# Two attention heads' blocks in one decode step: one row of the last weight matrix loaded ahead of the others, in uneven transfers

## The chip, the core and the metric

The kernel runs on one core of a Trainium2 chip. The time is device microseconds (us) of one execution, as the median of several runs; lower is better. A core has TensorE (PE, matrix products), VectorE (DVE), ScalarE (ACT), GpSimd (POOL), SyncE (SP, which here only issues transfers) and sixteen DMA engines that carry all transfers from the large memory (HBM) into the on-chip memory of 128 partitions.

## What is computed

Two independent attention blocks, A and B, each for one new token. Both have 32 query heads, 16 heads of keys and values, 8192 cached positions of 128 numbers; A looks at the last 2048 positions only (W), B at all.

```
q = (x @ wq)                      # 576 -> 32 x 128
scores = q . k * 128**-0.5        # over W (A) or 8192 (B) cached positions
p = softmax(scores)
o = p . v                         # 32 x 128
out = o.reshape(4096) @ wo        # 4096 -> 576
return concat([out_A, out_B])     # 1152 numbers, bf16
```

The inputs are bf16. The cached keys and values of B are the bulk of the bytes: some 67 MB of the 102.76 MB that the kernel reads.

## The kernel before

The program is written as a list of operations for each engine, with named dependences; the class `Prog` turns these into semaphores. The order on each engine is the order in which the operations are put down.

**Loads.** All large loads are issued by SP, in one order, into one ring of 72 x 1024 bf16 per partition (`place`, L167 to L185). Each load has a semaphore of its own out of 24 (`s_ld`), and waits only until the piece of the ring that it overwrites has been used. A load of 128 partitions increments its semaphore sixteen times. The order is: wq of A and B (L189 to L194), keys and values of the eight units (four of A, four of B; L219 to L222), then wo of A and of B (L224 to L231). Apart from them, ACT loads the two vectors x (one row each, L253), and SP stores the two halves of the result (L523).

**Units.** A unit is four heads of keys and values. For each, DVE transposes keys in slabs (L350), PE multiplies them by the queries (L367), the maximum and the exponentials follow (L382 to L406), and PE multiplies the probabilities by the values (L431). The code of unit i puts the transposes and scores of unit i + 1 ahead of the products with the values of unit i.

**The end.** After the last unit the sums are folded and divided (L482 to L499); the result `oP` holds, for each block, 32 columns of 128 numbers. The last product, with wo, is at L502 to L524. wo has 4096 rows of 576 numbers; partition p holds rows 32p to 32p + 31, and these are called here row 0 to row 31 of wo (one row in each partition is 1152 bytes). For each row k there are two matmuls with a column of `oP` as weights: 320 columns of the result, and the other 256. They go to four separate bands of one PSUM bank (partitions 0 and 32 for A, 64 and 96 for B), and each band sums over its 32 rows. `NWO` (L34) says in what pieces wo is loaded and multiplied: A's in one of 32 rows, B's in pieces of 17, 8, 4, 2 and 1 rows. The pieces of B are called wo1.0 to wo1.4, and the multiplications F1.0 to F1.4; each F waits for its own piece. After the last row of a block ACT and DVE copy the two parts out of PSUM (L519, L521) and SP stores them.

Of the kernel before, what the change touches and what calls it, by code (L numbers as in the profile page):

```python
# [11 lines left out]
HQ = 32  # L12
G = 16
DH = 128
DM = 576
# [5 lines left out]
NQ = G // 4  # L21
# [9 lines left out]
RING = 72 * 1024  # L31
NSEM = 24
NKT = 3
NWO = [[32], [17, 8, 4, 2, 1]]  # L34


class Prog:
# [9 lines left out]
    def op(self, eng, fn, deps=(), name=None):  # L47
        self.ops[eng].append((fn, tuple(deps), name, None))
        if name is not None:
            assert name not in self.where, name  # L50
            self.where[name] = (eng, len(self.ops[eng]) - 1)

    def load(self, eng, fn, sem, value, deps=(), name=None, step=16):
        self.ops[eng].append((fn, tuple(deps), None, (sem, step)))
        if name is not None:
            assert name not in self.dma, name
            self.dma[name] = (sem, value)
# [40 lines left out]
def bass_concat_heads__sliding_block_cached__gqa_block_cached__decode_kernel(nc, A_x, A_k_cache, A_v_cache, A_wq, A_wo,  # L98
                         B_x, B_k_cache, B_v_cache, B_wq, B_wo, out):
    xs, ks, vs = [A_x, B_x], [A_k_cache, B_k_cache], [A_v_cache, B_v_cache]  # L100
    wqs, wos = [A_wq, B_wq], [A_wo, B_wo]
# [42 lines left out]
    oP = nc.alloc_sbuf_tensor("oP", [128, 2, HQ], BF16)  # L144
# [9 lines left out]
    def view(t, free, offset, dims, parts=128, p0=0):  # L154
        return bass.AP(tensor=t, offset=p0 * free + offset, ap=[[free, parts], *dims])

    pg = Prog(nc)
    op, load = pg.op, pg.load
    s_x = [nc.alloc_semaphore("s_x%d" % i) for i in range(2)]
    s_ld = [nc.alloc_semaphore("s_ld%d" % i) for i in range(NSEM)]  # L160
    s_out = nc.alloc_semaphore("s_out")
    s_row = [nc.alloc_semaphore("s_row%d" % i) for i in range(2)]

# [3 lines left out]
    def place(size, uses, issue, name):  # L167
        if at[0] + size > RING:
            at[0] = 0
        lo, hi = at[0], at[0] + size  # L170
        at[0] = hi
        deps = []
        for r in list(live):
            if r[0] < hi and lo < r[1]:
                deps += r[2]
                live.remove(r)
        n = nload[0]
        nload[0] += 1
        if n >= NSEM:
            deps += uses_of[n - NSEM]  # L180
        uses_of.append(list(uses))
        live.append((lo, hi, list(uses)))
        t = ring[:, lo:hi]
        load("sp", lambda e: issue(e, t), s_ld[n % NSEM], 16 * (n // NSEM + 1), deps=deps, name=name)
        return t  # L185
# [35 lines left out]
            if 0 <= n < NU:  # L221
                load_kv(kind, n)  # L222

    wo_at = {}  # L224
    for P in range(2):
        k0 = 0
        for c, kk in enumerate(NWO[P]):
            src = wos[P].rearrange("(p k) n -> p (k n)", k=HQ)[:, k0 * DM:(k0 + kk) * DM]
            wo_at[P, c] = place(kk * DM, ["F%d.%d" % (P, c)], lambda e, t, src=src: e.dma_start(t, src),
                                "wo%d.%d" % (P, c))  # L230
            k0 += kk  # L231

    def slab(kind, i, s):

# [9 lines left out]
       deps=["id0"], name="ident")  # L244
# [15 lines left out]
    for c in range(2):  # L260
        op("dve", lambda e, c=c: e.tensor_reduce(par[:, c:c + 1], view(identf, 128, c, [[2, 64]]), AX.X, ALU.add),
           deps=["identf"], name="par%d" % c)
# [3 lines left out]
    for P in range(2):  # L266
        op("dve", lambda e, P=P: e.tensor_copy(  # L267
            view(xdup, 256, 128 * P, [[2, 64], [1, 2]], parts=1),
            view(xrow, 2 * DM, P * DM + 512, [[1, 64], [0, 2]], parts=1)), deps=["x%d" % P], name="xd%d" % P)
        for k in range(5):  # L270
            def mm(e, P=P, k=k):
                if k < 4:
                    lhsT = view(xrow, 2 * DM, P * DM + k, [[4, 128]], parts=1)
                else:
                    lhsT = xdup[0:1, P, :]
                return e.matmul(banks[2 * P + k // 4][:, (k % 4) * 128:(k % 4 + 1) * 128], lhsT=lhsT,  # L276
                                rhs=onesb[0:1, :], start=True, stop=True)
            op("pe", mm, deps=["x%d" % P, "onesb", "xd%d" % P], name="xT%d.%d" % (P, k))
        op("dve", lambda e, P=P: e.tensor_copy(
            xrep[:, P, 0:4, :].rearrange("p k m -> p (k m)"), banks[2 * P][:, :]), deps=["xT%d.3" % P], name="xr%d.0" % P)  # L280
        for c in range(2):
            op("dve", lambda e, P=P, c=c: e.tensor_scalar(
                xrep[:, P, 4 + c, :], banks[2 * P + 1][:, 0:128], par[:, c:c + 1], None, ALU.mult),
                deps=["xT%d.4" % P, "par%d" % c], name="xr%d.%d" % (P, 1 + c))
# [3 lines left out]
       deps=["identf"], name="clsb")  # L288
    op("dve", lambda e: e.tensor_reduce(clsa[:], view(identf, 128, 0, [[1, 8], [8, 16]]), AX.X, ALU.add),
       deps=["identf"], name="clsa")  # L290
    op("dve", lambda e: e.tensor_reduce(sel[:], view(identf, 128, 0, [[1, 32], [32, 4]]), AX.X, ALU.add),
       deps=["identf"], name="sel")
# [6 lines left out]
    for P in range(2):  # L299
        for n in range(8):  # L300
            u = 8 * P + n
            bank = banks[u % 4]

            def mm(e, P=P, n=n, bank=bank):
                for k in range(5):
                    if k < 4:
                        lhsT, o = xrep[:, P, k, :], wq_at[P, 0][:, k * w + n * 512:k * w + (n + 1) * 512]
                    else:
                        lhsT, o = xrep[:, P, 4 + n // 4, :], wq_at[P, 1][:, (n % 4) * 512:(n % 4 + 1) * 512]
                    ins = e.matmul(bank[:, :], lhsT=lhsT, rhs=o, start=(k == 0), stop=(k == 4))  # L310
                return ins
            op("pe", mm, deps=["wq%d.0" % P, "wq%d.1" % P] + XR + (["qe%d" % (u - 4)] if u >= 4 else []),
               name="qmm%d.%d" % (P, n))
            op("act", lambda e, u=u, bank=bank: e.activation(qsb[:, u % 4, :], bank[:, :], ACT.Copy),  # L314
               deps=["qmm%d.%d" % (P, n)] + (["qT%d" % (u // 2 - 2)] if u >= 4 else []), name="qe%d" % u)
            if n % 2:
                op("dve", lambda e, u=u, n=n: e.transpose(  # L317
                    ktb[:, (n - 1) * 512:(n + 1) * 512].bitcast(I32),
                    qsb[:, u % 4 - 1:u % 4 + 1, :].rearrange("p a n -> p (a n)").bitcast(I32)),
                    deps=["qe%d" % (u - 1), "qe%d" % u] + (["z0.%d" % i for i in range(4)] if P else []),  # L320
                    name="qT%d" % (u // 2))
        for b in range(4):
            if P == 1:
# [3 lines left out]
                    deps=["qT%d" % u for u in range(4, 8)] + ["zb0"], name="z1.%d" % b)  # L327
            else:
# [3 lines left out]
                    deps=["qT%d" % u for u in range(4)] + ["za0"], name="z0.%d" % b)  # L332
# [4 lines left out]
    k0 = [sum(nslab[:i]) for i in range(NU)]  # L337
# [117 lines left out]
    for i in range(NU):  # L455
        n = nslab[i + 1] if i + 1 < NU else 0
# [18 lines left out]
        for s in range(nslab[i]):  # L475
# [13 lines left out]
                                start=True, stop=True),  # L489
       deps=["lsel", "lselA", "nb%d" % last, "mr%d" % last], name="L")  # L490
# [3 lines left out]
        deps=["rl", "O%d" % last], name="on")  # L494
    op("dve", lambda e: e.transpose(oq[:].rearrange("p c k -> p (c k)"), on[:].rearrange("p c k -> p (c k)")),
       deps=["on"], name="oq")
    op("pe", lambda e: e.matmul(mb[:, 64:128], lhsT=perm[:, :], rhs=oq[:].rearrange("p c k -> p (c k)"),
                                start=True, stop=True), deps=["oq", "rl", "perm"], name="pm")
# [2 lines left out]

    fb = qb[0]  # L502
    for P in range(2):
        k0 = 0
        for c, kk in enumerate(NWO[P]):
            def mm(e, P=P, c=c, k0=k0, kk=kk):
                for k in range(kk):
                    for n in range(2):
                        r, lo, hi = 32 * (2 * P + n), n * N0, N0 + n * (DM - N0)
                        ins = e.matmul(fb[r:r + 1, 0:hi - lo], lhsT=oP[:, P, k0 + k:k0 + k + 1],  # L510
                                       rhs=wo_at[P, c][:, k * DM + lo:k * DM + hi],
                                       start=(k0 + k == 0), stop=(k0 + k == HQ - 1))
                return ins
            op("pe", mm, deps=["wo%d.%d" % (P, c), "oP", "exp%d" % (NQ - 2)], name="F%d.%d" % (P, c))
            k0 += kk
        done = "F%d.%d" % (P, len(NWO[P]) - 1)
        r, lo = 64 * P, P * DM

        load("act", lambda e, r=r, lo=lo: e.activation(outsb[0:1, lo:lo + N0], fb[r:r + 1, 0:N0], ACT.Copy),  # L519
             s_row[P], 2, deps=[done], name="f%d" % P, step=1)  # L520
        load("dve", lambda e, r=r, lo=lo: e.tensor_copy(outsb[0:1, lo + N0:lo + DM], fb[r + 32:r + 33, 0:DM - N0]),  # L521
             s_row[P], 2, deps=[done], step=1)
        load("sp", lambda e, lo=lo: e.dma_start(out[0, 0:1, lo:lo + DM], outsb[0:1, lo:lo + DM]),  # L523
             s_out, 16 * (P + 1), deps=["f%d" % P], name="out%d" % P)  # L524
# [31 lines left out]
```

## Time and profile before

| | |
|---|---|
| median of 3 runs | 246.21 us (246.15 to 246.38) |
| span of the profiled execution, first to last instruction | 245.2 us |
| bytes read from HBM | 102.76 MB, 419 GB/s over the span |
| PE busy | 172.3 us, 70% of the span |
| DVE busy | 129.1 us, 53% |
| ACT busy | 24.3 us, 10% |
| SP's issue of wo of A | at 208.37 us |
| SP's issues of the five pieces of wo of B | from 208.74 us, 2.33 us in all |
| from issue to landing: wo of A, pieces of B | 23.9 us; 29.3, 31.6, 32.5, 32.8, 32.6 us |

The span is that of one execution taken with the hardware profiler; the median of the timed runs is 1.0 us longer, which is what lies around the first and the last instruction. Busy times are sums over the span; they say how much an engine did, not what the end waited for. A transfer's time from issue to landing includes its time in the queue behind the transfers ahead of it.

### The profile page before, as it was taken

To read this page: it belongs to the slowest core of one execution; us is meant where nothing else is said; L and a number is where in the kernel's file an instruction comes from. 1 tells how busy PE (TensorE), PEld (TensorE's weight loads), DVE (VectorE), ACT (ScalarE), POOL (GpSimd) and SP (SyncE) were. 2 spreads that over 40 slices of the span, in tenths; PEclk is the share of its full clock that TensorE was granted. 3 is DMA by queue.
4 is the path that set the end of the run, shared out by engine and by line. 5 is a ranking of instruction groups with operands and counts; after the bars stand their busy time and mean duration, and the time that the engine had idled before them with its cause. 6 is when DMAs were issued, how large, how long until landed. Compare 5 with 4: busy or idle time off the path is not lost.

```text
span 245.2 us, 2253 instructions
## 1 busy us (share of the span) xinstructions
PE 172.3 (70%) x960; PEld 71.8 (29%) x961; DVE 129.1 (53%) x162; ACT 24.3 (10%) x52; POOL 8.2 (3%) x15
## 2 busy tenths in 40 slices
PE   0269967787867994889582869945579939257197
PEld 0124422224433222432130523211423213213154
DVE  0422547667789986699501699810679920500201
ACT  2004540021201000100000100000010000200001
POOL 8400000000000000000000000000000000000000
PEclk9999995789999997569957578989657985677559
DMA  7999999999999999998999999999999999999994
GB/s 267 420 457 410 437 428 425 433 428 457 440 430 387 468 428 428 452 470 385 406 428 425 438 476 428 438 406 425 438 466 460 395 406 430 428 438 409 430 407 158
DMA packets 4481, 102.90 MB, mean 420 GB/s; under 512 B 500, under 2 KB 632, under 8 KB 1144
## 3 DMA queue, kind: packets, MB, share of 16 engines
q1 hardware_dynamic: 4468, 102.76, 97.9%
q8 instruction: 7, 0.11, 0.2%
q14 instruction: 2, 0.02, 0.0%
q10 hardware_dynamic: 4, 0.00, 0.0%
HBM read 102.76 MB, written 0.00 MB: 419 GB/s over the span
## 4 chain that ended last, share of the span: by engine, by line
DMA 55%; PE 29%; DVE 12%; ACT 2%; issue 2%; SPq 0%; DVEq 0%
DMA ring<-in_B_v_cache_dram 40%; DMA ring<-in_A_wo_dram 10%; DVE ktb L350 9%; PE vb L431 8%; DMA ring<-in_A_wq_dram 5%; PE qb L367 5%; PE qb L510 5%; PE sb L310 5%; PE qb L310 4%; ACT psb L406 1%; DVE pta L414 1%; PE ob L447 1%; PE sb L367 1%; PE qb L359 1%; PE mb L397 1%
## 5 line engine op out<-in xcount | busy, mean ns | idle before, releaser
L350 DVE STREAM_TRANSPOSE ktb<-ring 128x1024 int32<-128x1024 int32 x80 | 92.8, 1211 | 29.5 <-DMA ring<-in_B_k_cache_dram 28.3
L367 PE MATMUL sb<-ktb,zb 128*128 128x512 bf16 x256 | 76.0, 437 | 23.7 <-DVE ktb L350 21.1
L367 PEld LDWEIGHTS sb<-ktb,zb 128*128 128x128 bf16 x256 | 23.4, 106 | 72.4 <-DVE ktb L350 45.9
L431 PE MATMUL vb<-ring,pts 128*32 128x512 bf16 x256 | 24.7, 567 | 18.5 <-DMA ring<-in_B_v_cache_dram 14.4
L367 PE MATMUL qb<-ktb,za 128*128 128x512 bf16 x64 | 19.4, 449 | 2.8 <-DVE ktb L350 2.8
L431 PEld LDWEIGHTS vb<-ring,pts 128*32 128x32 bf16 x256 | 9.0, 134 | 33.6 <-DMA ring<-in_B_v_cache_dram 16.7
L438 ACT ACTIVATE xo<-vb 128x512 f32<-128x512 f32 x8 | 4.8, 597 | 129.4 <-PE vb L431 129.4
L418 DVE STREAM_TRANSPOSE pts<-psb 32x512 bf16<-32x512 bf16 x16 | 11.3, 703 | 9.5 <-ACT psb L406 9.3
L510 PE MATMUL qb<-ring,oP 128*1 128x256 bf16 (+1 forms) x128 | 11.3, 340 | 4.0 <-DMA ring<-in_A_wo_dram 4.0
L317 DVE STREAM_TRANSPOSE ktb<-qsb 128x512 int32<-128x512 int32 x8 | 5.7, 711 | 15.0 <-ACT qsb L314 15.0
L310 PE MATMUL sb<-ring,xrep 128*128 128x512 bf16 x40 | 11.4, 442 | 2.7 <-DMA ring<-in_A_wq_dram 2.7
L447 PEld LDWEIGHTS ob<-sel,xo 128*128 128x128 f32 x64 | 10.9, 244 | 3.8 <-ACT xo L438 2.2
L447 PE MATMUL ob<-sel,xo 128*128 128x8 f32 x64 | 10.1, 285 | 1.2 <-ACT xo L438 1.2
L367 PEld LDWEIGHTS qb<-ktb,za 128*128 128x128 bf16 x64 | 6.1, 109 | 13.4 <-issue 5.8
L310 PE MATMUL qb<-ring,xrep 128*128 128x512 bf16 x39 | 9.5, 393 | 0.0
L510 PEld LDWEIGHTS qb<-ring,oP 128*1 128x1 bf16 x128 | 7.0, 93 | 8.3 <-DMA ring<-in_A_wo_dram 4.1
L521 DVE CAST outsb<-qb 1x256 bf16<-1x256 f32 x2 | 0.8, 420 | 14.7 <-PE qb L510 14.7
L491 DVE RECIPROCAL rl<-mb 128x64 f32<-128x64 f32 x1 | 0.6, 558 | 12.3 <-PE mb L488 12.3
L276 PE MATMUL sb<-onesb,xrow 1*128 1x128 bf16 x4 | 0.6, 298 | 9.2 <-DVE xdup L267 9.2
L392 DVE TENSOR_REDUCE mr<-mb 1x8 f32<-1x128 f32 x8 | 1.9, 240 | 9.5 <-PE mb L384 9.5
L310 PEld LDWEIGHTS sb<-ring,xrep 128*128 128x128 bf16 x40 | 4.3, 109 | 8.6 <-issue 5.3
L314 ACT ACTIVATE qsb<-sb 128x512 bf16<-128x512 f32 x8 | 4.8, 597 | 19.1 <-PE sb L310 19.1
(65 smaller groups left out, 68.8 us busy)
## 6 DMA issues: line engine op xcount, KB each, us to landing
ring<-in_B_k_cache_dram SPq DMA_DIRECT2D x8, 4096.0 KB, 24.5
ring<-in_A_k_cache_dram SPq DMA_DIRECT2D x4, 2048.0 KB, 30.5
ring<-in_A_v_cache_dram SPq DMA_DIRECT2D x4, 2048.0 KB, 25.4
ring<-in_B_v_cache_dram SPq DMA_DIRECT2D x2, 4096.0 KB, 23.8
ring<-in_A_wo_dram SPq DMA_DIRECT2D x1, 4608.0 KB, 23.9
ring<-in_A_wq_dram SPq DMA_DIRECT2D x1, 4096.0 KB, 12.5
ring<-in_B_wq_dram SPq DMA_DIRECT2D x1, 4096.0 KB, 22.6
ring<-in_B_wo_dram SPq DMA_DIRECT2D x1, 2448.0 KB, 29.3
```

The lines of the kernel that those rows point to most:

```text
L310: ins = e.matmul(bank[:, :], lhsT=lhsT, rhs=o, start=(k == 0), stop=(k == 4))
L314: op("act", lambda e, u=u, bank=bank: e.activation(qsb[:, u % 4, :], bank[:, :], ACT.Copy), deps=["qmm%d.%d" % (P, n)] + (["qT%d" % (u // ...
L317: op("dve", lambda e, u=u, n=n: e.transpose(ktb[:, (n - 1) * 512:(n + 1) * 512].bitcast(I32), qsb[:, u % 4 - 1:u % 4 + 1, :].rearrange("p ...
L350: op("dve", lambda e: e.transpose(kt.bitcast(I32), src.bitcast(I32)), deps=[landed] + (["S%d" % (k - NKT)] if k >= NKT else Z), name="T%d. ...
L359: e.matmul(bank[:, :], lhsT=mkl[:].rearrange("p a h r -> p (a h r)"), rhs=mkr[:].rearrange("p q h -> p (q h)"), start=True, stop=False)
L367: ins = e.matmul(bank[:, :], lhsT=lhsT, rhs=view(ktb, KT, (k % NKT) * SLAB + 64 * c + v, [[128, 16], [2, 32]]), start=(side == "B" and s = ...
L397: op("pe", lambda e: e.matmul(mb[:, 128:129], lhsT=mexp[0:1, :], rhs=onesf[0:1, 0:1], start=True, stop=True), deps=["mx%d" % i, "ones"], n ...
L418: op("dve", lambda e, b=b: e.transpose(view(pts, NB * 128, 2 * b, [[8, 16], [128, NB], [1, 2]], 32, 32 * b), psb[32 * b:32 * b + 32, :]), ...
L431: ins = e.matmul(vbank[i][32 * j:32 * j + 32, :], lhsT=lhsT, rhs=src[:, 512 * j:512 * j + 512], start=(s == 0), stop=(s == nslab[i] - 1))
L438: op("act", lambda e: e.activation(xo[:, c, :], vbank[i][:, :], ACT.Copy), deps=["V%d.%d" % (i, nslab[i] - 1)] + (["O%d" % (i - 1)] if i e ...
L447: ins = e.matmul(ob[:, at:at + 8], lhsT=xo[:, c, 128 * t:128 * t + 128], rhs=sel[:, 8 * t:8 * t + 8], start=(t == 0), stop=(t == 3))
L510: ins = e.matmul(fb[r:r + 1, 0:hi - lo], lhsT=oP[:, P, k0 + k:k0 + k + 1], rhs=wo_at[P, c][:, k * DM + lo:k * DM + hi], start=(k0 + k == 0 ...
```

## The change

B's wo is cut into six pieces instead of five. The first is row 31 alone, and it is put ahead of the others in the queue; then rows 0 to 15, 16 to 23, 24 to 27, 28 and 29, and 30. The rows, the bytes and the matmuls are the same. Row 31 is loaded by three transfers, of the partitions 0 to 39, 40 to 124 and 125 to 127; the first has the semaphore that `place` gives, the other two have new ones (`s_wox`), and F1.0 waits for all three. The sum in each band now begins with row 31: `start` and `stop` go by a count of the rows done.

```diff
-NWO = [[32], [17, 8, 4, 2, 1]]
+NWO = [[32], [1, 16, 8, 4, 2, 1]]
+XWO = [(0, 40), (40, 125), (125, 128)]
...
+    s_wox = [nc.alloc_semaphore("s_wox%d" % i) for i in range(len(XWO) - 1)]
...
+        rows = wos[P].rearrange("(p k) n -> p (k n)", k=HQ)
         for c, kk in enumerate(NWO[P]):
-            src = wos[P].rearrange("(p k) n -> p (k n)", k=HQ)[:, k0 * DM:(k0 + kk) * DM]
-            wo_at[P, c] = place(kk * DM, ["F%d.%d" % (P, c)], lambda e, t, src=src: e.dma_start(t, src),
-                                "wo%d.%d" % (P, c))
-            k0 += kk
+            split = P == 1 and c == 0
+            wo_k[P, c] = HQ - 1 if split else k0
+            src = rows[:, wo_k[P, c] * DM:(wo_k[P, c] + kk) * DM]
+
+            def issue(e, t, src=src, part=XWO[0] if split else (0, 128)):
+                return e.dma_start(t[part[0]:part[1], :], src[part[0]:part[1], :])
+            t = wo_at[P, c] = place(kk * DM, ["F%d.%d" % (P, c)], issue, "wo%d.%d" % (P, c))
+            if split:
+                for i, part in enumerate(XWO[1:]):
+                    load("sp", lambda e, t=t, src=src, part=part: e.dma_start(
+                        t[part[0]:part[1], :], src[part[0]:part[1], :]), s_wox[i], 16, name="wox%d" % i)
+            else:
+                k0 += kk
...
-                                       start=(k0 + k == 0), stop=(k0 + k == HQ - 1))
+                                       start=(done + k == 0), stop=(done + k == HQ - 1))
...
+            op("pe", mm, deps=["wo%d.%d" % (P, c), "oP", "exp%d" % (NQ - 2)] +
+               ["wox%d" % i for i in range(len(XWO) - 1) if (P, c) == (1, 0)], name="F%d.%d" % (P, c))
```

More of the change, by code (lines that the diff above doesn't have):

```diff
@@ L222, in bass_concat_heads__sliding_block_cached__gqa_block_cached__decode_kernel @@
                 load_kv(kind, n)
-    wo_at = {}
+    wo_at, wo_k = {}, {}
     for P in range(2):
         k0 = 0
+        rows = wos[P].rearrange("(p k) n -> p (k n)", k=HQ)
         for c, kk in enumerate(NWO[P]):
-            src = wos[P].rearrange("(p k) n -> p (k n)", k=HQ)[:, k0 * DM:(k0 + kk) * DM]
-            wo_at[P, c] = place(kk * DM, ["F%d.%d" % (P, c)], lambda e, t, src=src: e.dma_start(t, src),
-                                "wo%d.%d" % (P, c))
-            k0 += kk
+            split = P == 1 and c == 0
[10 more added lines that the diff above has]
+                k0 += kk
     def slab(kind, i, s):
@@ L503, in bass_concat_heads__sliding_block_cached__gqa_block_cached__decode_kernel, with mm @@
     for P in range(2):
-        k0 = 0
+        done = 0
         for c, kk in enumerate(NWO[P]):
-            def mm(e, P=P, c=c, k0=k0, kk=kk):
+            def mm(e, P=P, c=c, k0=wo_k[P, c], kk=kk, done=done):
                 for k in range(kk):
@@ L511, in mm @@
                                        rhs=wo_at[P, c][:, k * DM + lo:k * DM + hi],
-                                       start=(k0 + k == 0), stop=(k0 + k == HQ - 1))
+                                       start=(done + k == 0), stop=(done + k == HQ - 1))
                 return ins
-            op("pe", mm, deps=["wo%d.%d" % (P, c), "oP", "exp%d" % (NQ - 2)], name="F%d.%d" % (P, c))
-            k0 += kk
+            op("pe", mm, deps=["wo%d.%d" % (P, c), "oP", "exp%d" % (NQ - 2)] +
+               ["wox%d" % i for i in range(len(XWO) - 1) if (P, c) == (1, 0)], name="F%d.%d" % (P, c))
+            done += kk
         done = "F%d.%d" % (P, len(NWO[P]) - 1)
```

## The prediction

> **What bounds the kernel now.** I read the page first, then the chain of work that ended last, then windows of 0.25 us over the last microseconds, then the timeline of the end.
>
> ```profile
> DMA  7999999999999999998999999999999999999994
> ...
> q1 hardware_dynamic: 4468, 102.76, 97.9%
> ...
> DMA 55%; PE 29%; DVE 12%; ACT 2%; issue 2%; SPq 0%; DVEq 0%
> ```
>
> The sixteen DMA engines are busy from end to end: 102.76 MB in 245.2 us. Per engine that is 102.76 MB / 16 / 240 us of busy time, some 26.8 KB/us, so a row of wo in one partition (1152 B) is worth 0.043 us of one engine. Nothing the compute engines do in the middle can move the time by much; only the start and the end can. The chain ends so:
>
> ```profile
> 208.37 23.91 DMA ring<-in_A_wo_dram
> 232.28 0.04 issue
> 232.32 11.31 PE qb L510 x94
> 243.63 0.02 issue
> 243.65 0.43 ACT outsb L519
> ```
>
> The chain puts the last 11.31 us down to TensorE. The windows show that DMA is not far from it:
>
> ```profile
> 240.75:241.00 0.25, 0.25 (x8) 0.17 (x4) 0.00 (x0) 0.00 (x0) 0.00 (x0) 1.00 0.78 304
> 241.00:241.25 0.25, 0.25 (x8) 0.15 (x4) 0.00 (x0) 0.00 (x0) 0.00 (x0) 1.00 0.50 198
> ...
> 242.00:242.25 0.25, 0.25 (x6) 0.17 (x4) 0.00 (x0) 0.00 (x0) 0.00 (x0) 1.00 0.42 152
> 242.25:242.50 0.25, 0.25 (x7) 0.25 (x6) 0.00 (x0) 0.00 (x0) 0.00 (x0) 1.00 0.22 78
> 242.50:242.75 0.25, 0.25 (x8) 0.20 (x3) 0.00 (x0) 0.00 (x0) 0.00 (x0) 1.00 0.08 28
> ```
>
> The last three columns are granted clock, DMA share, GB/s. The share falls to one half at 241.0, stays there for more than a microsecond, and is nearly gone at 242.5: **half of the DMA engines are done about 1.3 us ahead of the other half**, although each has the same 8 of 128 partitions of every load. The trace's record of semaphore increments (one from each engine that carried a part) gives the same for the last piece, wo1.4: seven at 240.92 to 241.41, one at 241.72, eight from 242.25 to 243.27. Why some are late is also in it: the page's third part has 7 packets on queue 8, 16 KB each, the fetches of instructions. At each of their times (38.9, 70.8, 100.0, 132.1, 169.3, 206.7, 236.1 us) one engine's own packets stop for 1.05 to 1.15 us, and its landings stay late from there to the end. Two shorter fetches (66.1 and 182.3) hit two more. No engine is hit twice, so seven are left unhurt; among these, by the continuity of its packets, is the one that carried the two one-row loads of x. The slowest, 2.35 us behind the first, was a little late from the start and was then hit at 132.1.
>
> TensorE at the end:
>
> ```profile
> 242.96 0.09 PEld L510 LDWEIGHTS qb<-ring,oP 128*1 128x1 bf16 x4 [0.21 <-DMA ring<-in_B_wo_dram]
> 243.31 0.08 PEld L510 LDWEIGHTS qb<-ring,oP 128*1 128x1 bf16 x2 [0.26 <-DMA ring<-in_B_wo_dram]
> 243.65 0.43 ACT L519 ACTIVATE outsb<-qb 1x320 bf16<-1x320 f32 x1 [3.47 <-PE qb L510]
> ```
>
> Its last two pieces wait for data (they land at 242.92 and 243.27, starts 0.04 us later). But the 320-wide matmuls, one for each row, start every 0.135 us without a hole from the first row of B at 239.01 until 242.81. With no wait at all the 32nd row would start at 239.01 + 31 x 0.1355 = 243.21, against 243.31 now. So **in this execution TensorE is only 0.10 us behind DMA as the bound**.
>
> **The change, part by part.** All sizes are from this trace's packets; starts of 1152 B packets on one engine lie 0.047 us apart, those of the 17-row packets 0.725, of the 8-row ones 0.344, so a 16-row packet comes to 0.683 (0.0368 us per KB of difference).
>
> *The 17-row piece loses a row.* Every engine has 8 packets, each shorter by 0.042: minus 0.34 us on all sixteen.
>
> *The row comes back in three transfers ahead of it.* Both shapes that the trace has are split evenly (128 partitions: sixteen increments, 8 rows each; the one-row load of x: one). 85 can be shared evenly by 5 or by 1 of at most sixteen, 3 by 3 or 1, 40 by 10, 8 or fewer. I take the widest. Then 17 rows on each of five engines, 4 on each of ten, 1 on each of three, and with nested sets: 22 rows for three engines, 21 for two, 4 for five, none for six. Net of the 0.34: +0.69, +0.65, -0.15, -0.34 us. If the odd transfers went to one engine, that one would have 85 x 0.047 - 0.34 = +3.65; these are the two ends. [...]
>
> *What it does to the end.* If no engine that was hit hard is among the five, the slowest lands 0.34 earlier (0.15 if it is in the middle five), at 242.93; the burdened ones end at 241.41 + 0.69 = 242.10, with room. Then the last row starts at the later of 242.97 and TensorE's own 243.21: **minus 0.10 us in this execution**, and what is late next is TensorE. That cover depends on the clock: granted 0.50 until 238.21, 1.00 after, and the record changes only in steps of 3.41 us. A.wo's 32 rows start every 0.267 us at half clock and 0.135 at full. If the step fell 0.5 us earlier, B's rows would start 0.25 us earlier and the whole 0.34 would show; if later, none. [...]
>
> *At no cost:* three more issues on SP, 0.47 us each (2.33 us for five at 208.74). They sit in front of wo1.1 to wo1.4 and the two stores of out; the pieces land 24 to 33 us after their issue and the first store is issued at 240.20, so 1.4 us is hidden by A.wo's transfer. Without that cover it would cost 1.4. Two more semaphore waits on TensorE at B's first piece, one more at its second: landed by 237.8, and met while the band of A's 320-wide matmuls, which ends at 239.71, still has rows to run; bound 0 to 0.1, taken as 0. A.wo's landing at 232.28, which starts TensorE's stretch, is ahead of the new transfers in the queue. The number of matmuls, their shapes and the tail after the last are as before.
>
> *Sum:* span 245.2 and about 1.0 around it make the median of 246.21. Minus 0.10 (TensorE bound) to minus 0.34 (DMA bound) gives 246.11 to 245.87; I take **246.0**.
>
> **Rivals.**
> 1. *A hit engine is among the five burdened, though not the slowest.* Late by 1.6 to 1.96 us, plus 0.69, it lands 2.3 to 2.65 after the first, against 2.35 now: 246.15 to 246.5. For it: only seven of sixteen are unhurt, and five drawn by lot would nearly always hold a hit one. [...]
> 2. *Slower: the slowest engine itself is burdened.* It lands at 243.27 + 0.69 = 243.96, TensorE waits there: 246.9. It decides when the engine at 2.35 gets over 8 rows more than it gives up.
> 3. *The odd transfers run on one engine.* +3.65 on an unhurt one (0 to 0.49) gives 3.7 to 4.1 against 2.35: 247.5 to 248.0. For it: x's load does run on one. Against: 85 has another even division.
> 4. *No relief:* TensorE is the bound in most timed runs, or the relieved engines aren't the late ones: 246.2.
> 5. *More than 0.34:* the gain would have to come from TensorE starting B's rows earlier as well, with a clock step earlier than before by chance of the runs: 245.7.
>
> **How the numbers follow.** Forecast 0.56, rival 1 0.13, rival 2 0.12, rival 3 0.06, rival 4 0.06, rival 5 0.07. 0.2% is 0.49 us, about what a measurement of this kernel can tell from no change. The forecast, rival 1 and rival 4 are within it: same 0.75. Rival 5 is faster, 0.07; rivals 2 and 3 are slower, 0.18. The range from 245.7 to 246.65 holds the forecast and rivals 1, 4 and 5, with 0.15 above rival 1 for its bounds; rivals 2 and 3 are left out.
>
> **What would show it.** Right: in windows of 0.25 us the DMA share after 241 falls from more than half to nothing by about 242.5 instead of 242.9; the last LDWEIGHTS waits less than 0.26 or not at all, and the 320-wide starts of B run without a hole to 243.2. Wrong: a plateau of one to five engines (share 0.06 to 0.3) after 243, a wait for in_B_wo ahead of the first or second piece of B, or a last wait that has grown.

## The result, and the profile after

The changed kernel takes 247.03 us in the median (246.91 to 247.59, five runs), the kernel before 246.22 (246.15 to 246.38): a ratio of 1.0033, 95% interval 1.0022 to 1.0043. It is 0.8 us slower, where 0.2 us less was forecast, and outside the range of 245.7 to 246.65.

The DMA row of the page is the same as before and the queue's share differs by 0.2 points; these two rows hide the loss. The third line, the shares of the chain, does change (DMA was 55%), but not by the change's doing, as is shown below:

```profile
DMA  7999999999999999998999999999999999999994
...
q1 hardware_dynamic: 4614, 102.76, 98.1%
...
DMA 70%; PE 18%; DVE 9%; SPq 1%; issue 1%; ACT 1%; DVEq 0%
```

The chain has changed its end: TensorE's 11.31 us are gone from it, and a load of B's wo stands there, with short pieces of TensorE after it.

```profile
209.44 33.09 DMA ring<-in_B_wo_dram
242.54 0.04 issue
242.58 0.70 PE qb L522 x7
243.29 0.00 issue
243.29 0.68 PE qb L522 x5
243.97 0.02 issue
243.99 0.43 ACT outsb L532
```

The timeline of TensorE's weight loads (start, busy time, in brackets the idle time before and what ended it) shows that it now waits for every piece of B after the 16 rows:

```profile
241.21 0.90 PEld L522 LDWEIGHTS qb<-ring,oP 128*1 128x1 bf16 x16 [0.70 <-DMA ring<-in_B_wo_dram]
242.58 0.36 PEld L522 LDWEIGHTS qb<-ring,oP 128*1 128x1 bf16 x8 [0.47 <-DMA ring<-in_B_wo_dram]
243.29 0.09 PEld L522 LDWEIGHTS qb<-ring,oP 128*1 128x1 bf16 x4 [0.35 <-DMA ring<-in_B_wo_dram]
243.64 0.08 PEld L522 LDWEIGHTS qb<-ring,oP 128*1 128x1 bf16 x2 [0.27 <-DMA ring<-in_B_wo_dram]
```

The clock's step came at 236.61 here instead of 238.21, so A's rows were done earlier and DMA alone sets the end. That holds without the change too: in a second profile of the kernel before (before_again, below) the step came at 235.69, DMA has 70% of the chain, a load of B's wo stands at its end, and TensorE waits for every piece after the first. Two of these four waits:

```profile
240.72 0.90 PEld L510 LDWEIGHTS qb<-ring,oP 128*1 128x1 bf16 x16 [0.62 <-DMA ring<-in_B_wo_dram]
242.08 0.36 PEld L510 LDWEIGHTS qb<-ring,oP 128*1 128x1 bf16 x8 [0.46 <-DMA ring<-in_B_wo_dram]
```

What the change moved is the last landing: 243.60, against 243.27 and 243.11 in the two profiles of the kernel before. The windows of 0.25 us (last columns: clock, DMA share, GB/s) have no plateau at one half any more; the share holds up longer and ends later:

```profile
241.00:241.25 0.25, 0.04 (x2) 0.04 (x4) 0.00 (x0) 0.00 (x0) 0.00 (x0) 1.00 0.97 387
...
242.00:242.25 0.25, 0.25 (x7) 0.08 (x1) 0.00 (x0) 0.00 (x0) 0.00 (x0) 1.00 0.66 249
242.25:242.50 0.25, 0.20 (x2) 0.00 (x0) 0.00 (x0) 0.00 (x0) 0.00 (x0) 1.00 0.57 212
242.50:242.75 0.25, 0.17 (x4) 0.14 (x6) 0.00 (x0) 0.00 (x0) 0.00 (x0) 1.00 0.43 152
```

So the ends of the engines were evened out a little (the sixteen landings of the last piece lie 1.99 us apart instead of 2.35), and the more even end still lies after the old one. The engines must have become slower somewhere. Windows of 4 us find the place. First the kernel after, then the experiment one_piece (below), which reads the same rows in the same order:

```profile
225.00:229.00 4.00, 2.40 (x10) 2.21 (x10) 1.03 (x3) 0.40 (x1) 0.00 (x0) 0.50 1.03 442
229.00:233.00 4.00, 0.58 (x5) 0.36 (x7) 0.23 (x1) 0.00 (x0) 0.00 (x0) 0.50 0.89 300
```

```profile
225.00:229.00 4.00, 2.40 (x10) 2.21 (x10) 1.03 (x3) 0.40 (x1) 0.00 (x0) 0.50 1.03 442
229.00:233.00 4.00, 1.16 (x10) 0.88 (x12) 0.23 (x1) 0.00 (x0) 0.00 (x0) 0.50 0.88 369
```

**The share is the same, 0.89 and 0.88, but the bytes are not: 300 GB/s against 369.** So in these two windows the busy share counts a packet that takes longer as fully busy, whether its bytes move or wait. The loss is 69 GB/s for 4 us, 0.28 MB; at 427 GB/s, the middle value of the 40 slices on the page after, that is 0.65 us. The trace's packet records say the same: between 229 and 233 us seven of the last 36 KB packets of A.wo, as many as there are late engines, take 1.62 to 1.88 us instead of 1.37, those of 16 rows 0.70 to 1.03 instead of 0.686, the small ones up to 0.106 instead of 0.051. What packets took above the median of their size, counted where it is over 4% and summed from 20 us on, is called their excess below: 15.2 us against 4.5 in the kernel before; the difference, spread over sixteen engines, is 0.67 us each.

The increments of the semaphores also tell how the three transfers were shared: besides one at once from the queue itself, the 40 partitions gave ten, the 85 five, the 3 three. That step was right.

### The profile page after: what moved, and what is told of

The parts are those of the page before. It is cut to its first block, busy times and chain, and to the rows that moved or that the text cites. A ratio compares the mean times of both kernels' runs of the same rounds, so it can differ in the third digit from the quotient of the medians.

```text
span 245.6 us, 2258 instructions
## 1 busy us (share of the span) xinstructions
PE 171.4 (70%) x961; PEld 72.0 (29%) x961; DVE 129.0 (53%) x162; ACT 24.3 (10%) x52; POOL 8.1 (3%) x15
## 4 chain that ended last, share of the span: by engine, by line
DMA 70%; PE 18%; DVE 9%; SPq 1%; issue 1%; ACT 1%; DVEq 0%
DMA ring<-in_B_v_cache_dram 39%; DMA ring<-in_B_wo_dram 13%; DMA ring<-in_B_k_cache_dram 12%; DVE ktb L362 8%; PE vb L443 7%; DMA ring<-in_A_wq_dram 5%; PE sb L322 4%; PE qb L322 4%; PE sb L379 1%; PE ob L459 1%; PE qb L522 1%; SPq L236 1%; ACT psb L418 0%; DVE ktb L329 0%; DVE pta L426 0%
## 5 line engine op out<-in xcount | busy, mean ns | idle before, releaser
L379 PEld LDWEIGHTS sb<-ktb,zb 128*128 128x128 bf16 x256 | 22.6, 105 | 72.2 <-DVE ktb L362 47.7
L443 PE MATMUL vb<-ring,pts 128*32 128x512 bf16 x256 | 24.0, 553 | 20.9 <-DMA ring<-in_B_v_cache_dram 16.9
L459 PEld LDWEIGHTS ob<-sel,xo 128*128 128x128 f32 x64 | 12.5, 277 | 4.0 <-ACT xo L450 2.4
L522 PE MATMUL qb<-ring,oP 128*1 128x256 bf16 (+1 forms) x128 | 10.8, 324 | 3.9 <-DMA ring<-in_A_wo_dram 3.4
L459 PE MATMUL ob<-sel,xo 128*128 128x8 f32 x64 | 11.7, 310 | 1.2 <-ACT xo L450 1.2
```

The lines of the kernel that those rows point to most:

```text
L379: ins = e.matmul(bank[:, :], lhsT=lhsT, rhs=view(ktb, KT, (k % NKT) * SLAB + 64 * c + v, [[128, 16], [2, 32]]), start=(side == "B" and s = ...
L443: ins = e.matmul(vbank[i][32 * j:32 * j + 32, :], lhsT=lhsT, rhs=src[:, 512 * j:512 * j + 512], start=(s == 0), stop=(s == nslab[i] - 1))
L459: ins = e.matmul(ob[:, at:at + 8], lhsT=xo[:, c, 128 * t:128 * t + 128], rhs=sel[:, 8 * t:8 * t + 8], start=(t == 0), stop=(t == 3))
```

## The experiments

Theories: **P**, a guess, that the way into a partition is a path which several engines can share, so that an engine writing to another's partitions slows it; **B**, the prediction's, that only the rows on each engine count (rival 1: a hit engine among the five); **Q**, that the order, the sixth piece or its semaphores cost the time; and **H**, that the distance of the rows in HBM does. The edits are against the changed kernel, and of the longer ones only the lines that matter are shown. The ratios are each to runs of the kernel before on the same chip.

**The kernel before again** (no edit).

> The kernel before, unchanged, as a second look at its profile. All theories: 246.2 us, within 0.1 of itself; the sixteen landings of A.wo stay 1.9 to 2.4 us apart; no packet of the last loads takes over 4% longer than others of its size, except right after an instruction fetch. It also gives the span beside the time of the same execution.

246.34 against 246.34, ratio 1.0001 (0.9993 to 1.0010). No stretched packets but after the instruction fetches. A.wo's landings lie 2.10 us apart. Its profiled execution took 246.41 us with a span of 245.1: 1.3 lie around the span, and so it is in the other profiled runs (246.93 and 245.6 after).

**one_piece: the order alone.**

```diff
-XWO = [(0, 40), (40, 125), (125, 128)]
+XWO = [(0, 128)]
```

> Row 31 first, but in one transfer of 128 partitions. [...] Theory Q (the order, the sixth piece and its semaphores cost the time): 247.0.

246.35, ratio 0.9999 (0.9991 to 1.0008). Q, with its 247.0, falls: row 31 first, six pieces and the new order cost nothing. By B and by P nothing costs time here either. What is left is the three uneven transfers.

**halves: even load, other partitions.**

```diff
-XWO = [(0, 40), (40, 125), (125, 128)]
+XWO = [(0, 64), (64, 128)]
```

> Row 31 first, in two transfers of 64 partitions: every engine has 8 rows of it, as in one transfer, but other partitions than usual. Theory B: equal load, so 246.2. [...] Theory Q: 247.0 or a little less.

247.38, ratio 1.0046 (1.0032 to 1.0060): more than the change itself, though each engine has its 8 rows. B alone can't give this; P has the sign. The window shows the same loss behind a high share:

```profile
225.00:229.00 4.00, 1.56 (x11) 1.29 (x11) 1.25 (x4) 0.49 (x1) 0.00 (x0) 0.88 1.01 433
229.00:233.00 4.00, 0.00 (x0) 0.00 (x0) 0.00 (x0) 0.00 (x0) 0.00 (x0) 0.50 0.93 313
```

**own_way: the change's load on the engines, destinations four partitions apart.** The rows go to spare memory, one partition for each engine, four apart, in four transfers; nothing reads them there, and B's row 31 is multiplied by row 31 of A's wo instead. Of the edit only the four destinations are shown, with the rows of each:

```diff
+bass.AP(tensor=za, offset=0, ap=[[4 * NQ * 4 * ZA, 10], [DM, 4], [1, DM]])   # 40 rows
+bass.AP(tensor=ktb, offset=0, ap=[[4 * kt, 5], [DM, 10], [1, DM]])           # 50 rows
+bass.AP(tensor=ring, offset=RING - 4096, ap=[[4 * RING, 5], [DM, 7], [1, DM]])  # 35
+bass.AP(tensor=xrep, offset=0, ap=[[4 * 1536, 3], [1, DM]])                  # 3
```

> The same rows as in the change on the same numbers of engines (ten with 4, five with 17, three with 1; the 17 in two transfers of 10 and 7), but they are put into spare memory of the partitions 0, 4, 8 and so on, one partition for each engine, so that hardly any engine writes to a path of another. B's row 31 is multiplied by row 31 of A's wo instead of its own. Theory B: same load on the same engines, so the time of the change, 246.9 to 247.1. Theory P: no stretched packets in A.wo; what is left is the burden of the one hit engine (0.65 for its 21 rows, less than it was late), so 246.2 to 246.6. Theory Q: 247.0.

246.27, ratio 0.9996 (0.9987 to 1.0005). The same rows on the same numbers of engines cost nothing here, so B falls. The packets' excess is 4.8 us, close to the 4.5 of the kernel before, and the bytes are back:

```profile
225.00:229.00 4.00, 2.45 (x11) 2.26 (x11) 1.03 (x3) 0.31 (x1) 0.00 (x0) 0.50 1.03 442
229.00:233.00 4.00, 1.18 (x10) 0.84 (x12) 0.22 (x1) 0.00 (x0) 0.00 (x0) 0.50 0.88 364
```

**neighbours: own_way with a step of one partition instead of four.**

```diff
-ap=[[4 * kt, 5], [DM, 10], [1, DM]]
+ap=[[kt, 5], [DM, 10], [1, DM]]
```

and likewise in the other three destinations.

> As the run own_way (same rows read, same engines with 21, 22 and 4 of them, B's row 31 multiplied by A's), but the ten, five and three destinations are the partitions 0 to 9, 0 to 4 and 0 to 2 instead of every fourth. One number in each of four access patterns differs. [...] Theory B, or any in which the destination doesn't matter: as own_way, 246.1 to 246.5.

248.96, ratio 1.0108 (1.0093 to 1.0123). The same rows, the same numbers of engines, and 2.7 us more than own_way, through the destination alone, which has P's sign. The last piece lands 3.30 us after its first engine's part, against 1.97 in own_way. B's range, 246.1 to 246.5, is missed by 2.5; how the cost adds up isn't shown. The windows, and the waits that follow:

```profile
225.00:229.00 4.00, 1.56 (x11) 1.29 (x11) 1.25 (x4) 0.33 (x1) 0.00 (x0) 0.85 1.01 433
229.00:233.00 4.00, 0.00 (x0) 0.00 (x0) 0.00 (x0) 0.00 (x0) 0.00 (x0) 0.50 0.93 236
```

```profile
243.31 0.90 PEld L532 LDWEIGHTS qb<-ring,oP 128*1 128x1 bf16 x16 [0.74 <-DMA ring<-in_B_wo_dram]
244.69 0.36 PEld L532 LDWEIGHTS qb<-ring,oP 128*1 128x1 bf16 x8 [0.48 <-DMA ring<-in_B_wo_dram]
```

**sixteens: even load, sixteen neighbouring partitions at a time.**

```diff
+XWO = [(i, i + 16) for i in range(0, 128, 16)]
```

> Row 31 first, in eight transfers of 16 partitions: each engine has one row of each, 8 in all, as in the kernel before. Theory B: equal load, 246.2, the five more issues are hidden. [...]

247.12, ratio 1.0029 (1.0019 to 1.0040). Slower at equal load, as in halves: P has the sign, B doesn't. Most small packets took their 0.051 us (none over 0.088); the large packets beside and behind them carried the wait (excess 16.1 us in all). So the delay need not show in the records of the small packets themselves.

**near_source: rows that lie together in HBM.**

```diff
+            if split:
+                src = wos[P][128 * 31:128 * 32, :]
```

> As the change, but the three transfers read 128 rows of B's wo that lie one behind the other in HBM instead of every 32nd row. So B's row 31 is multiplied by other rows than its own. Theory P: nothing changes, 246.9 to 247.1, packets stretched as in the change. Theory H (the distance of the rows in HBM slows the small packets): packets of 51 ns again, and 246.2 to 246.6. Theory B: 246.9 to 247.1.

This kernel leaves out B's row 31 and uses other rows of wo for it. 246.94, ratio 1.0026 (1.0017 to 1.0035), excess 15.2 us as in the change. H falls.

**unhurt: the extra rows on the three engines that no long fetch had hit.**

```diff
+XWO = [(0, 51), (51, 115), (115, 128)]
```

> Row 31 first, in transfers of 51, 64 and 13 partitions: by the increments seen in the change that is 17 rows on three engines, 4 on all sixteen and 1 on thirteen. The three take 22 rows; none of them had been hit hard. The fourth and fifth, one of which was hit, take 5. Theory B: the hit engine gives up 3 rows instead of taking 13, all late engines give up 3 or 4: 246.05 to 246.2. Theory P: packets of A.wo are stretched as in the change, only the hit engine's burden (about 0.3 at the end) is gone: 246.5 to 246.8.

246.93, ratio 1.0025 (1.0015 to 1.0035): no better than the change, against both expectations. No engine sticks out at the end (the last two land 1.78 and 1.77 after the first; in the change 1.99, then 1.70), so the hit engine's burden is gone; but the excess is 17.5 us instead of 15.2. By P this is the transfer of 64 partitions that all sixteen engines share.

**left_out: no row 31 at all.**

```diff
+            if split:
+                wo_at[P, c] = None
+                continue
```

> Row 31 of B's wo isn't loaded at all; B's row 31 is multiplied by row 31 of A's wo. Every engine then has 8 rows fewer, 0.34 us. All theories: no stretched packets; TensorE has a limit of its own, 0.1 behind in the profile of before, so 245.85 to 246.1, which is the most that unloading any engine by its 8 rows could give.

Row 31 of A's wo is multiplied in its place. 246.11 against 246.32, ratio 0.9990 (0.9981 to 0.9999). That is the most there was to win by unloading any engine by its 8 rows.

**one_engine: 127 partitions and 1.**

```diff
+XWO = [(0, 127), (127, 128)]
```

> Row 31 first, in transfers of 127 partitions and of 1. By the increments seen so far (the engines of a transfer share its partitions evenly; x's one row has one engine), 127 rows can only be shared by one engine. It has 128 x 0.047 - 0.34 = 5.7 us more, less the 1.5 to 2.1 by which it was ahead of the slowest: 249.7 to 250.6 by theory B. Theory P: the same and something more, because that engine's packets meet each path's own traffic in turn: 249.7 to 251.5. If the transfers were spread over the sixteen engines all the same: 246.3.

251.07, ratio 1.0193 (1.0176 to 1.0210), within P's range and above B's. One engine does carry it: a single increment at the end. That engine lands 4.0 us after the first, the next 2.1. Part of the time is something else. The issue of the 127 partitions took SP 0.33 us (SPq L236 at 207.96, start and time taken), but the issue of the single partition right behind it (L240) held SP for 22.16 us, and the later pieces could be given only then,

```profile
207.96 0.33 SPq L236 DMA_DIRECT2D ring<-in_B_wo_dram  x1
208.34 22.16 SPq L240 DMA_DIRECT2D ring<-in_B_wo_dram  x1
230.54 2.35 SPq L236 DMA_DIRECT2D ring<-in_B_wo_dram  x5
```

so this run doesn't separate P from B.

## Why the prediction was wrong

*What bounds the kernel: right.* Half of the engines were late because of instruction fetches (a stop of 1.00 to 1.08 us at each of seven; the last section has the steps), and the end is set by the last landing, with TensorE close behind. The experiment left_out puts the worth of the row at 0.2 us, between the two ends of 0.10 and 0.34.

*How the transfers are shared: right.* Ten, five and three engines, by the increments. That the smaller sets lie within the larger ones was an assumption of the prediction: the increments don't name engines. Nor did the trace before show that the five would be clear of a hit engine, on which the forecast and its 0.56 rest; in own_way (A.wo's landing at 231.16, below) one of them was a hit one.

*The row's price on an engine, 0.047 us: right where nothing interferes.* In own_way A.wo's landing on the hit engine among the five is 231.16. By the prediction's own sum its last part should land 10.98 later (as from A.wo to the end in before_again, 232.13 to 243.11) plus 0.65: 242.79. Measured: 242.79, the last of the sixteen, with two more within 0.06. The increments don't name engines; that the last one is the hit one is read from the packets, each of which starts where the one before it on its engine ended. So rival 1's condition was so (a hit engine, not the slowest, is burdened), and by itself it costs nothing in the time: 0.9996.

***The step that failed: "Net of the 0.34: +0.69, +0.65, -0.15, -0.34 us".*** It takes each engine's time as the sum of its own packets. But the row for the relieved engines' partitions still has to arrive; now other engines bring it, while the late ones are still busy with A.wo. (Which partitions an engine serves isn't recorded; the reading rests on the runs below.) The seven late engines landed the last piece of V 1.19 to 1.88 us after the first engine, and A.wo, the next load, 1.61 to 2.46 after it: taken in order, 0.42 to 0.63 us were lost within A.wo, before a single row was saved; then the 0.34 came back. In before, before_again, one_piece and left_out the same seven lag no more than 0.02 us further at A.wo than at V, in own_way 0.05; in halves, sixteens, near_source and unhurt it is 0.34 to 0.80, in neighbours 0.97 to 1.16. The price of writing where another engine is writing, 0.67 us for each engine by the packets' excess, was no term of the sum at all, neither in the forecast nor in a rival. The runs halves (even load, slow) and own_way against neighbours (same load, only the destination differs) show that it hangs on the destination.

How far the destinations have to lie apart is shown at two points: a step of four partitions cost nothing (own_way, 0.9996), a step of one 2.7 us more (neighbours against own_way). No run tries a step of two or three.

*Rival 2 gave 246.9, by chance.* Its mechanism didn't happen: the slowest engine of A.wo (2.46 us behind) isn't among the five, whose late one was 1.61 behind.

*The frame was 0.3 off.* About 1.3 us lie around the span, not 1.0, so by this the execution that I read took some 246.5, one of the longer ones of the kernel before.

*TensorE's cover: right, and it fell away as described.* The clock's step lay 1.6 us earlier in the profile after, and the full delay of DMA showed. The term of minus 0.10 belonged to one execution: before_again, with its step at 235.69, has no such cover. Where the timed runs took the step isn't shown.

What stays open: how much of the 0.8 us is the stretch of the late engines and how much the hit engine's burden on top of it. In the change's profile that engine did land last, by 0.28 us; the next one, at 243.32, is 0.21 behind before_again's last although it had 0.34 less to do. The run unhurt was to separate the two and didn't, since its excess is larger. Also, the two profiled executions (246.93 and before_again's 246.41) differ by 0.52 us, so some 0.3 of the medians' 0.8 stands in neither trace. And the path itself isn't seen in any record: shown is that the destination decides, not by what part of the chip.

## What to carry to other kernels

As these runs bear it out, an uneven split of a load over DMA engines moves bytes between engines, while the partitions that they go to stay the same; and while the moved rows were being written, the late engines' packets of A.wo took 1.62 to 1.88 us instead of 1.37. What decided was the destination: with the same rows and the same numbers of engines, 246.27 us with a step of four partitions and 248.96 with a step of one. None of the four splits tried here (40, 85 and 3; halves; sixteens; 51, 64 and 13) helped the lagging engines; each cost 0.6 to 1.0 us. So before such a split is costed, where each engine writes is to be looked at beside the packets of each engine. And a high DMA share is no sign of progress (0.89 with 300 GB/s, 0.88 with 369): compare GB/s at equal share.

## What the runs showed of the hardware that was not expected

- Fetches of instructions held a DMA engine: at each of the seven of 16 KB in the kernel before, one engine's own packets stopped for 1.00 to 1.08 us from one's end to the next one's start (the prediction gives 1.05 to 1.15), and its loads stayed late to the end. The sixteen landings of a load show it step by step. Up to the first fetch, at 38.9 us, all lie within 0.84 us and fifteen of them within 0.5; in the next load one lands 1.77 behind; by 209.3 us seven land 1.3 to 2.3 behind, and after the fetch at 236.1 eight. The engine that was 0.82 behind before the fetch at 132.1 was 2.34 behind after it: 1.5 us, more than the stop; where the rest comes from isn't shown.
- Two transfers of 64 partitions for one of 128, 147 KB in all, cost 1.0 us (247.38 in halves against 246.35 in one_piece) beside a busy stream, with the same load on every engine.
- In one_engine the issue of one partition, right behind that of 127 partitions, held SP for 22.16 us, where that of the 127, and that of the 128 of A.wo, took 0.33 each. By the increments all the 127 rows were one engine's; why the next issue had to wait isn't shown.
